# Zeros ahead of the first h, x loaded by head on two queues, half the state later: the head of a fused attention and gated-MLP kernel

## The chip, the cores and the metric

One core of one Trainium2 chip. The metric is the device time of one execution in microseconds (us), the median of several runs. Ratios between two kernels are the mean time of one kernel's runs over that of the other's of the same rounds, so they are not quite the ratios of the medians quoted beside them.

## The reference, cut to what matters

```python
def _attn_ref(x, state):                      # x (8, 8, 512, 64), state (8, 8, 32, 64)
    scores = scale * np.matmul(x, state.transpose(0, 1, 3, 2))
    a = softmax(scores);   xread = np.matmul(a, state)
    scores2 = scale * np.matmul(state, x.transpose(0, 1, 3, 2))
    a2 = softmax(scores2); sread = np.matmul(a2, x)
    return np.concatenate([xread, sread], axis=2)

def _moe_ref(x, w_in, w_out):                 # 4352 tokens, 512 -> 2048 -> 512
    h = x @ w_in
    g = h * np.cos(h)
    return g @ w_out
```

(Softmax is abbreviated.) The weights come as 64-bit floats. The kernel turns them into 32-bit floats by handling their halves as integers, in the steps called 1, 2, a, b, c, d below.

## The kernel before: the parts concerned

Every engine works through a fixed order. A sample is one of the eight x[b]; before TensorE can make the first h of a sample, x must be loaded, turned by TensorE, multiplied with the state (scores), passed through a softmax on VectorE and ScalarE, and the first weights must be converted. Names used below: st is the state as loaded and stT the state turned and scaled; xT is x turned; aT is the result of the first softmax, which the first h needs; exp2 is the exponential of the second softmax (scores2), on ScalarE; q holds ScalarE's and VectorE's steps from h to g; a gate is the last of these (g_all from h and q). One `matmul` of the program shows as one or two passes in the trace, so a product of zeros is two passes. "By head" means by attention head; "the head of the kernel" is its first 130 us.

```python
    def load_x(b):                                   # four quarters of the tokens
        src = x[b].rearrange("h (c p) d -> c p h d", p=P)
        for c in range(NC):
            nc.sync.dma_start(out=x_b[:, c], in_=src[c])
    load_x(0)
    for k in range(NK):                              # the whole state, 8 loads of 64 KB
        for j in range(2):
            queue = nc.scalar if j == 0 else nc.gpsimd
            queue.dma_start(out=st[Ns * k:Ns * k + Ns, :, D * j:D * j + D], in_=st_src[j, k])
    # ... cut ...
        def all_tokens(self):                        # 16 transposes, k-major
            for k in range(NK):
                for c in range(NC):
                    self.turn_x(k, c, xp[k])
                # copied to xT[:, k] by ScalarE (k even) or VectorE (k odd)
    # ... cut ...
    fetch(3)                                         # first three weight loads, sync queue
    a0.all_tokens()
    states(0, at[0]); states_kept(0, at[0])          # the state's transposes, kept by VectorE
    a0.scores()
    convert(0, "12ab")                               # 1, 2: ScalarE; a, b, c: VectorE; d: GpSimd
    a0.max1(); a0.spread1(); a0.shift()
    convert(1, "12")
    a0.exp1()
    convert(0, "cd")
    a0.sums()
    convert(1, "abcd")                               # load 1: d on VectorE too
    a0.spread1()
    convert(2, "12")
    a0.norm1()                                       # aT is done: the first h can start
    a0.products(0, MAIN, 0, HC)
    # ... then 8 samples of 16 steps each: hidden (h), gate (q, g), output (o)
```

## Time and profile before

| | before |
|---|---|
| time, median of 6 runs | 821.85 us (821.24 to 821.96) |
| span in the profile | 819.9 us, granted clock 0.997 |
| TensorE busy | 765.5 us, 93% |
| scores start | 15.49 us |
| first h starts | 29.23 us |
| TensorE bound from | about 130 us |

In the busy rows of a page each digit is the busy share of a fortieth of the span, in tenths. A line of the chain of waits is start, duration, what; a line of the timeline is start, duration, engine, source line, operation, output and inputs, and in brackets how long the engine had been idle and what ended that.

### The profile page before, as it was taken

How to read it: one execution, taken by the hardware profiler on the slowest of the kernel's cores; microseconds unless marked ns; L12 is line 12 of the kernel's file. 1: busy time of each engine (PE TensorE's matmuls, PEld its weight loads, DVE VectorE, ACT ScalarE, POOL GpSimd, SP SyncE). 2: the span in 40 equal slices, each digit the busy share in tenths (PEclk: the TensorE clock that was granted, in tenths of full speed). 3: DMA queues.
4: the chain of work that ended last, by engine and by line, in shares of the span. 5: the costliest groups of instructions: out<-in, count | busy, mean ns of one | idle time of the engine just before them, and what ended most of it. 6: DMA issues, size and time to landing. Idle time of an engine off the chain costs nothing.

```text
span 819.9 us, 7479 instructions
## 1 busy us (share of the span) xinstructions
PE 765.5 (93%) x2720; PEld 345.0 (42%) x2720; DVE 434.6 (53%) x672; ACT 397.9 (49%) x644; POOL 175.6 (21%) x117
## 2 busy tenths in 40 slices
PE   3569688989999999999999999999999999999997
PEld 2133233434444444444444444444344444455554
DVE  2799897653355435863454456743554355432431
ACT  2568675564447344644455454634473445322222
POOL 1134236877100000154000000451000002620200
PEclk9999999999999999999999999999999999999999
DMA  6574450102000211030010311120000112200021
GB/s 154 179 203 158 153 154 0 27 0 52 1 13 14 52 26 26 13 65 0 1 26 1 64 21 19 26 52 0 14 14 0 27 26 50 79 0 14 13 39 38
DMA packets 110500, 37.18 MB, mean 45 GB/s; under 512 B 102464, under 2 KB 102464, under 8 KB 110464
## 3 DMA queue, kind: packets, MB, share of 16 engines
q1 hardware_dynamic: 109248, 36.19, 18.8%
q10 hardware_dynamic: 1088, 0.26, 0.2%
q8 instruction: 21, 0.34, 0.2%
q0 software_dynamic: 128, 0.26, 0.2%
q14 instruction: 15, 0.12, 0.1%
HBM read 27.79 MB, written 8.91 MB: 45 GB/s over the span
## 4 chain that ended last, share of the span: by engine, by line
PE 78%; DVE 12%; ACT 7%; issue 1%; DMA 1%; POOL 0%; SPq 0%; DVEq 0%; POOLq 0%
PE o L489 42%; PE h L424 25%; PE at L276 4%; PE o L606 3%; DVE q L433 2%; PE at L363 2%; ACT q L439 1%; DVE g_all L445 1%; PE at L249 1%; ACT q L438 1%; DVE w_in L211 1%; DVE w_out L211 1%; DVE xT L296 1%; DVE aT L340 1%; DMA x_b<-in_x_dram 1%
## 5 line engine op out<-in xcount | busy, mean ns | idle before, releaser
L424 PE MATMUL h<-aT,sw 128*128 128x512 f32 x512 | 244.0, 599 | 17.9 <-DVE g_all L445 14.1
L489 PE MATMUL o<-g_all,w_out 128*128 128x512 f32 x512 | 236.5, 598 | 5.5 <-DVE sw L403 2.9
L430 ACT ACTIVATE q<-h 128x512 f32<-128x512 f32 (+1 forms) x144 | 82.2, 571 | 269.6 <-PE h L424 269.6
L451 POOL TENSOR_TENSOR g_all<-g_all 128x512 f32<-128x512 f32 x80 | 112.1, 1424 | 460.1 <-DVE g_all L445 454.5
L433 DVE SCALAR_TENSOR_TENSOR q<-q,h 128x512 f32<-128x512 f32 (+1 forms) x144 | 94.3, 655 | 208.0 <-ACT q L430 208.0
L489 PE MATMUL o<-g_all,s 128*128 128x512 f32 x384 | 177.3, 598 | 0.0
L445 DVE TENSOR_TENSOR g_all<-h,q 128x512 f32<-128x512 f32 (+1 forms) x144 | 94.8, 658 | 139.7 <-ACT q L439 139.4
L424 PEld LDWEIGHTS h<-aT,sw 128*128 128x128 f32 x512 | 96.6, 191 | 145.5 <-issue 109.3
L489 PEld LDWEIGHTS o<-g_all,w_out 128*128 128x128 f32 x512 | 93.6, 190 | 127.3 <-issue 119.8
L438 ACT ACTIVATE q<-q 128x512 f32<-128x512 f32 (+1 forms) x144 | 87.6, 608 | 103.6 <-DVE q L433 103.6
L489 PEld LDWEIGHTS o<-g_all,s 128*128 128x128 f32 x384 | 70.3, 190 | 88.4 <-issue 83.6
L439 ACT ACTIVATE q<-q,halfpi 128x512 f32<-128x512 f32 (+1 forms) x144 | 100.5, 698 | 4.5
L222 POOL TENSOR_TENSOR w_out<-w_out,s 128x1024 int32<-128x1024 int32 x10 | 23.8, 2385 | 87.5 <-DVE w_out L216 76.3
L451 DVE TENSOR_TENSOR g_all<-g_all 128x512 f32<-128x512 f32 x48 | 33.2, 692 | 1.6
L424 PE MATMUL h<-sT,w_in 128*128 128x256 f32 x128 | 30.2, 379 | 0.0
L405 ACT COPY sw<-at 128x512 f32<-128x512 f32 x48 | 25.7, 588 | 9.0 <-PE at L276 9.0
L606 PE MATMUL o<-w_out,g_all 128*128 128x512 f32 x64 | 29.6, 592 | 0.0
L222 POOL TENSOR_TENSOR w_in<-w_in,s 128x1024 int32<-128x1024 int32 (+1 forms) x9 | 18.0, 2000 | 53.8 <-DVE w_in L216 53.8
L424 PEld LDWEIGHTS h<-sT,w_in 128*128 128x128 f32 x128 | 24.3, 190 | 10.1 <-issue 6.7
L495 DVE SCALAR_TENSOR_TENSOR held<-o,held 128x512 f32<-128x512 f32 x40 | 25.5, 681 | 3.7 <-PE o L489 3.7
L276 PE MATMUL at<-w_in,stT 64*32 64x512 f32 x384 | 26.1, 601 | 0.0
L276 PE MATMUL o<-w_in,stT 64*32 64x512 f32 (+1 forms) x144 | 13.0, 606 | 13.3 <-POOL w_in L222 11.1
(79 smaller groups left out, 468.4 us busy)
## 6 DMA issues: line engine op xcount, KB each, us to landing
out_dram<-ot SPq DMA_DIRECT2D x136, 64.0 KB, 2.0
x_b<-in_x_dram SPq DMA_DIRECT2D x32, 256.0 KB, 4.5
g_all<-in_moe_w_out_dram SPq DMA_DIRECT2D x8, 1024.0 KB, 5.0
g_all<-in_moe_w_in_dram SPq DMA_DIRECT2D x6, 1024.0 KB, 5.3
g_all<-in_moe_w_in_dram SPq DMA_DIRECT2D x4, 512.0 KB, 7.0
x_b<-in_moe_w_out_dram SPq DMA_DIRECT2D x1, 1024.0 KB, 6.3
xT<-in_moe_w_out_dram SPq DMA_DIRECT2D x1, 1024.0 KB, 8.3
s<-in_state_dram ACTq DMA_DIRECT2D x4, 64.0 KB, 5.1
```

The lines of the kernel that those rows point to most:

```text
L222: engine.tensor_tensor(bits, bits, e.bitcast(I32), op=ALU.add)
L276: nc.tensor.matmul(out=(to or at)[j][Ns * k:Ns * k + Ns, 0:n], lhsT=w[D * j:D * j + D, self.b, Ns * k:Ns * k + Ns], rhs=r(slice(D * j, D * ...
L405: nc.scalar.copy(dst, to[j][:, 0:c1 - c0])
L424: nc.tensor.matmul(out=t.hp, lhsT=t.lhs(i), rhs=t.rhs(i), start=(i == 0), stop=(i == t.kn - 1))
L430: nc.scalar.activation(t.q, t.hp, func=ACTF.Copy, bias=MAGIC)
L433: nc.vector.scalar_tensor_tensor(out=t.q, in0=t.q, scalar=MAGIC, in1=t.hp, op0=ALU.subtract, op1=ALU.subtract)
L438: nc.scalar.activation(t.q, t.q, func=ACTF.Abs)
L439: nc.scalar.activation(t.q, t.q, func=ACTF.Sin, bias=halfpi, scale=-TWO_PI)
L445: nc.vector.tensor_tensor(t.g, t.hp, t.q, op=ALU.mult)
L451: engine.tensor_tensor(out, a, b, op=ALU.subtract)
L489: nc.tensor.matmul(out=acc[bank][ch], lhsT=w[:, i, P * ch:P * ch + P], rhs=g.g, start=(i == 0), stop=(i == NH - 1))
L606: nc.tensor.matmul(out=acc[MAIN][i], lhsT=t.g[:, P * i:P * i + P], rhs=w_out[:, :, t.f, :], start=(n == 0), stop=(n == NF - 1))
```

## The change

Its intent: have x and the needed part of the state earlier, work on each pair of heads as it lands, use VectorE's gap before the softmax sums for the second weight load, and keep TensorE's clock up ahead of the first h.

```diff
-    def load_x(b):
-        src = x[b].rearrange("h (c p) d -> c p h d", p=P)
-        for c in range(NC):
-            nc.sync.dma_start(out=x_b[:, c], in_=src[c])
-    load_x(0)
+    def load_x(b, queues):
+        src = x[b].rearrange("h (c p) d -> p c h d", p=P)
+        for h in range(H):
+            queues[h % 2].dma_start(out=x_b[:, :, h], in_=src[:, :, h])
+    zeros = g_all[:, 0]
+    nc.vector.memset(zeros, 0.0)
+    load_x(0, (nc.sync, nc.scalar))
...
+    def load_state(half, queues):                    # 4 of 8 samples, 8 loads of 32 KB
+        ...
+                queues[j].dma_start(out=st[..., b, ...], in_=st_src[j, k, :, b])
+    load_state(0, (nc.scalar, nc.gpsimd))
...
-            nc.vector.tensor_scalar(dst, dst, 2.0 ** -15, None, op0=ALU.max)
+            engine = nc.gpsimd if i == 1 else nc.vector
+            engine.tensor_scalar(dst, dst, 2.0 ** -15, None, op0=ALU.max)
...
-            engine = nc.vector if i == 1 else nc.gpsimd
-            engine.tensor_tensor(bits, bits, e.bitcast(I32), op=ALU.add)
+            n = 1 if i < 4 else 2
+            for j in range(n):
+                r = slice(m * j // n, m * j // n + m // n)
+                nc.gpsimd.tensor_tensor(bits[:, r], bits[:, r], e.bitcast(I32)[:, r], op=ALU.add)
...
     fetch(3)
+    load_state(1, (nc.sync, nc.sync))
+    warm(2, at[0])                                   # products of zeros
     a0.all_tokens()
     states(0, at[0]); states_kept(0, at[0])
     a0.scores()
+    warm(6, acc[SIDE][1])
     convert(0, "12ab")
+    convert(1, "12a")
     a0.max1(); a0.spread1(); a0.shift()
-    convert(1, "12")
     a0.exp1()
     convert(0, "cd")
+    convert(1, "bcd")
     a0.sums()
-    convert(1, "abcd")
     a0.spread1()
```

More of the change, by code (lines that the diff above doesn't have):

```diff
@@ L102 @@
     stT = consts.tile([P, B, P], F32)
-    def load_x(b):
-        src = x[b].rearrange("h (c p) d -> c p h d", p=P)
-        for c in range(NC):
-            nc.sync.dma_start(out=x_b[:, c], in_=src[c])
-    load_x(0)
-    st_src = state.rearrange("b (k j) n d -> j k n b d", j=2)
-    for k in range(NK):
-        for j in range(2):
-            queue = nc.scalar if j == 0 else nc.gpsimd
-            queue.dma_start(
-                out=st[Ns * k:Ns * k + Ns, :, D * j:D * j + D],
-                in_=st_src[j, k])
+    def load_x(b, queues):
[5 more added lines that the diff above has]
+    load_x(0, (nc.sync, nc.scalar))
+    st_src = state.rearrange("b (k j) n d -> j k n b d", j=2)
+    def load_state(half, queues):
+        b = slice(4 * half, 4 * half + 4)
+        for k in range(NK):
+            for j in range(2):
+                queues[j].dma_start(
+                    out=st[Ns * k:Ns * k + Ns, b, D * j:D * j + D],
+                    in_=st_src[j, k, :, b])
+    load_state(0, (nc.scalar, nc.gpsimd))
     at = [aps.tile([P, S], F32, name=f"at{j}") for j in range(2)]
@@ L220, in convert_part @@
         else:
-            engine = nc.vector if i == 1 else nc.gpsimd
-            engine.tensor_tensor(bits, bits, e.bitcast(I32), op=ALU.add)
+            n = 1 if i < 4 else 2
+            for j in range(n):
+                r = slice(m * j // n, m * j // n + m // n)
+                nc.gpsimd.tensor_tensor(bits[:, r], bits[:, r],
+                                        e.bitcast(I32)[:, r], op=ALU.add)
     sT = consts.tile([P, NK, B, Ns], F32)
@@ L414, in part @@
         if (name, args) == ("reads", (1,)) and b + 1 < B:
-            load_x(b + 1)
+            load_x(b + 1, (nc.sync, nc.sync))
     class Tile:
@@ L646, in tiles, with warm @@
             yield t
+    def warm(n, to):
+        for _ in range(n):
+            nc.tensor.matmul(out=to, lhsT=zeros[:, 0:P], rhs=zeros, start=True,
+                             stop=True)
     fetch(3)
+    load_state(1, (nc.sync, nc.sync))
+    warm(2, at[0])
     a0 = attn[0] = Attention(0)
```

## The prediction

> **What bounds the kernel now.** I read the busy row by slices first, then the chain that ended last in order of time, then the instructions of the first 130 us, then the same window cut into stretches.
>
> ```profile
> PE   3569688989999999999999999999999999999997
> DVE  2799897653355435863454456743554355432431
> ...
> PE 78%; DVE 12%; ACT 7%; issue 1%; DMA 1%; POOL 0%; SPq 0%; DVEq 0%; POOLq 0%
> ```
>
> A slice is 20.5 us. From the seventh slice on (about 130 us) TensorE is the bound: it works 632.83 of the 640 us after 180. The change hardly touches that part; it can only move it earlier as a whole. What can be won lies before 130 us, where TensorE is a third to two thirds busy. The chain of waits there starts so (start us, us, what):
>
> ```profile
> 3.05 7.64 DMA x_b<-in_x_dram
> 10.68 0.04 issue
> 10.73 3.04 PE o L249 x13
> 13.76 0.87 PE at L129 x4
> 14.63 0.02 issue
> 14.65 0.70 DVE stT L135
> 15.36 0.14 issue
> 15.49 2.06 PE at L276 x16
> 17.55 1.31 DVE m L290 x2
> ```
>
> The end hangs on the last quarter of x (landed at 10.7), then on 13 transposes that all waited for it, the state's transposes, the scores, and then VectorE without a hole until the first h:
>
> ```profile
> 22.57 1.30 DVE L290 TRANSPOSE_TENSOR_REDUCE m<-aT 128x16 f32<-128x512 f32 x2 [0.53 <-ACT aT L317]
> ...
> 24.39 0.36 DVE L211 TENSOR_SCALAR w_in<-w_in 128x512 f32<-128x512 f32 x1
> 24.79 0.43 DVE L213 TENSOR_SCALAR w_in<-w_in 128x512 int32<-128x512 int32 x1
> 25.25 0.69 DVE L216 SCALAR_TENSOR_TENSOR w_in<-g_all,w_in 128x512 int32<-128x512 int32 x1
> 25.98 0.69 DVE L222 CUSTOM_DVE_ANT_0 w_in<-w_in,s 128x1024 uint16<-128x1024 uint16 x1
> ...
> 27.86 1.23 DVE L340 TENSOR_TENSOR aT<-aT,xT 128x1024 f32<-128x1024 f32 x1
> ...
> 29.23 5.52 PE L424 MATMUL h<-aT,sw 128*128 128x512 f32 x8 [1.43 <-DVE aT L340]
> ```
>
> The four lines at 24.39 to 26.67 are the second weight load's conversion, standing between the softmax sums and the division; VectorE stood idle 0.53 us just before the sums, for the exponential. The first h matmuls: 8 take 5.52 us, while later four take 1.98 us, so some five of them ran at half speed.
>
> From 29 to 130 us the chain goes through VectorE, ScalarE and GpSimd in turn (all three run fixed orders), TensorE seldom. One group stands out:
>
> ```profile
> L211 DVE TENSOR_SCALAR w_in<-w_in x10: 363/682/2396, 15.3 to 83.2; 128x1024 f32<-128x1024 f32 x6, 128x512 f32<-128x512 f32 x4
> ```
>
> The same instruction takes 0.68 us alone and up to 2.4 us beside GpSimd's add: at 42.76 it took 2.37 us, ending 0.55 us after the add (42.21, 2.37 us).
>
> **What the Trainium skill says.** "TensorE: Matmul & The Clock Gate", Part 1: the array runs at half rate when it was idle and speeds up after about 3.4 us of sustained work. The trace agrees: 0.85 us apart at first, 0.43 us from 33.3, some 4 us in. "SBUF — State Buffer", Who interferes with whom: a VectorE instruction in a two-port mode, or with two SBUF inputs, and a GpSimd one exclude each other for the whole of the first to start. L211's 2.37 us shows it. "DMA: Bandwidth & Descriptors", Issuing engines are not separate DMA queues: a second issuing engine saves only issue time. In the stretches 2 to 9.5 us the 16 engines show a share of 1.02 to 1.32 at 230 to 182 GB/s, so they were full; I count nothing for the second queue as such.
>
> **The change part by part.**
>
> 1. Half of the state later. Until 9.5 us the stretches moved 1.57 MB (2 us each at 230, 214 and 206 GB/s, 1.5 us at 182), exactly x (1.05) and state (0.52), and x was seen 1.2 us after. Now x must share only with GpSimd's quarter of the state, 0.13 MB (ScalarE's quarter is queued behind its x): 1.18 MB at the same 213 GB/s is 5.5 us from 2.0, so 7.5, and seen at 8.75. Gain 1.9 us, an estimate. The first weights are then seen at about 10.9.
>
> 2. By head. A pair of heads gives four transposes at once; after the last pair only 4 of 0.234 us remain where 13 did: 9 x 0.234 = 2.1 us. So the scores start at about 11.5 instead of 15.49, and end at 13.5 instead of 17.53. ScalarE issues four x loads and four state loads first (0.55 us each, 4.4 us), then loads its table (1.28 us); it is free by 6.5, before its first copy.
>
> 3. Second conversion in gaps. Before, from the end of the scores to the end of L340 it is 29.09 - 17.53 = 11.56 us. Its max goes to GpSimd, its add too; shift (0.43) and xor (0.69) go before the sums, of which the exponential's wait hides 0.53 us. 0.36 + 0.43 + 0.69 + 0.69 with gaps (2.2) goes out of the path and 0.6 comes in: 1.6 us gained. But both adds (1.27 us each) now run on GpSimd just when VectorE does the shift, the xor and the small add after the sums (L332), which need the same port; each can be held up to 1.27 us. Laying them in order by "who comes first keeps it" gives an end between 9.95 and 11.3 us after the scores. I take 10.7: gain 0.9 us.
>
> 4. Zeros. Two products (four passes of 0.85 us at the slow clock) run at about 1.3 to 4.7 us, while x is awaited: free. Six (12 passes) start behind the scores, some five to seven at 0.85 and the rest at 0.43: about 7.5 us, until 21. The first real products can start when the first add ends, about 20, and the second half needs the second add, about 22; I count no delay. The first h then runs at full speed, saving 5 x 0.43 = 2.1 us of TensorE. But that isn't on the path: h was ready at about 32.6, ScalarE took it only at 33.42, behind exp2, which hangs on VectorE. I count 0. If the two early products keep the clock up through the scores, those take 1.09 instead of 1.96 us: 0.87 us at one chance in three, 0.3 us.
>
> 5. The add of the 14 full loads, and of the two late ones, in halves. Each now costs 2 x 1.27 instead of 2.37 us. A waiting L211 gets the port after 1.26 us. At 186.09 a tiny VectorE add took 0.36 us beside nine GpSimd instructions in a row, so VectorE does get in at such a border. Five L211 (42.76, 48.52, 56.92, 108.20, 126.56) came early enough in the add to profit. If VectorE then keeps the port for L213 too, each saves 1.0 us, less about 1.5 us where the chain hangs on the add itself (47.74 to 50.12): 3 us gained. If GpSimd gets it back in between, L213 waits for the second half and each loses 0.24 us, and that add ends 0.8 us later: 2 us lost. I take 0.5 us gained.
>
> 6. x loads of later samples: eight issues of about 0.4 us in place of four of 0.58, asked for at 52.76 and used at 61.93: hidden.
>
> Sum: 1.9 + 2.1 + 0.9 + 0.3 + 0.5 = 5.7 us. The first h should start at about 24.2 instead of 29.23. As every later step up to 130 us hangs on the same orders, and the weight loads (5 us) are asked for steps ahead, I let nearly all of it through and take off 0.4 us for what is lost on the way: 821.8 - 5.3 = 816.5.
>
> **Rivals.** (a) The transfer is hidden or the state becomes the wait: st now lies behind x in ScalarE's queue, and if it lands after 10 us, the state's transposes wait. For it: 0.13 MB more at 213 GB/s is 0.6 us. Against it: it is used only after x's last transposes, 0.94 us later. It would take 1 us: 817.5. (b) The conversions become the wait: L211 of load 0 stands in VectorE's order before the max, so weights landing after 12.5 would hold the softmax, and both adds on GpSimd hold L332. It would leave only parts 1 and 2, half eaten: 819. (c) Halving goes badly, or the slow clock falls elsewhere. At 50.16 eight matmuls took 1.93 instead of 1.06 us after a hole of 3.6 us; with a later add the hole grows: 819 to 820. (d) Everything goes well, the port stays with VectorE and the clock stays up: 811 to 813. (e) The zeros delay the real products: their 12 passes at 0.85 us would end at 23.7, a micro-second or two late: 818.
>
> **Range and chances.** The head gives 3 to 6 us, the halves -2 to +3: 812.5 to 819.5. For over 2% it would have to be under 805.4, more than the head has holes for; slower than 838 nothing suggests. Faster 0.02, same 0.97, slower 0.01.
>
> **What would show it.** Part 1: last x seen at 8 to 9.5 us. Part 2: four transposes after it, scores starting near 11.5. Part 3: L340 ending 10 to 11.3 us after the scores. Part 4: h at 0.43 us a pass, and ScalarE's first q still behind exp2. Part 5: L211 near 1.2 us or less where it took 2.4, and L213 either at 0.69 or at 1.9 us. Wrong I am, if the lead at the first h is not the lead at 130 us and at the end.

## More of the kernel before

The source lines of the changed kernel are shifted: its L264 is L249 of before (x's transposes), L138 was L129 (the state's), L291 was L276 (scores and weight products), L221, L223, L226, L236 were L211, L213, L216, L222 (steps a, b, c, d), L305 was L290 (max), L355 was L340 (aT), L439 was L424 (h). L667 is the new product of zeros.

## The result, and the profile after

The changed kernel takes 820.74 us (820.2 to 821.5, 6 runs) against 821.85; the ratio is 0.9989, with a 95% interval of 0.9976 to 1.0002. The forecast was 816.5 in 812.5 to 819.5. So 1.1 us came instead of 5.3, and the measured median lies outside the range. The interval includes 1, so even the 1.1 us is not clear of the noise.

The chain of waits of the changed kernel shows where the head now hangs:

```profile
1.85 5.22 DMA x_b<-in_x_dram
7.07 0.02 issue
7.09 0.32 ACTq L123
7.41 0.04 issue
7.45 4.94 DMA s<-in_state_dram
12.39 0.14 issue
12.52 1.10 PE at L138 x4
...
14.49 2.06 PE at L291 x16
```

x is no longer the wait. ScalarE's state loads stand behind x in its queue. In the chain the issue at 7.09 follows the landing of a load of x at 7.07; the last of them goes out at 7.45, takes 4.94 us for 32 KB, and lands at 12.39. TensorE had turned the last of x long before, as the timeline of the changed kernel shows in its first line here:

```profile
8.43 0.66 PE L264 MATMUL o<-ident,x_b 128*128 128x128 f32 x4 [0.66 <-DMA x_b<-in_x_dram]
...
20.96 0.42 DVE L223 TENSOR_SCALAR w_in<-w_in 128x512 int32<-128x512 int32 x1
...
21.41 1.65 DVE L226 SCALAR_TENSOR_TENSOR w_in<-g_all,w_in 128x512 int32<-128x512 int32 x1
...
26.22 1.23 DVE L355 TENSOR_TENSOR aT<-aT,xT 128x1024 f32<-128x1024 f32 x1
...
27.59 6.51 PE L439 MATMUL h<-aT,sw 128*128 128x512 f32 x8 [2.42 <-DVE aT L355]
...
54.26 2.93 POOL L236 TENSOR_TENSOR w_out<-w_out,s 128x512 int32<-128x512 int32 x2 [5.39 <-DVE w_out L226]
54.76 1.32 DVE L221 TENSOR_SCALAR w_in<-w_in 128x1024 f32<-128x1024 f32 x1
56.11 1.64 DVE L223 TENSOR_SCALAR w_in<-w_in 128x1024 int32<-128x1024 int32 x1
```

The only transposes left after the last of x are four (0.66 us), as forecast. The xor of load 1 (L226) takes 1.65 us instead of 0.69, because it stands beside GpSimd's add. The first h runs no faster: 6.51 us for the eight passes that took 5.52. And with the add in halves the max (L221) gets in after 1.3 us instead of 2.4, but then the shift (L223) waits for the second half, 1.64 us instead of 0.69.

Then the clock. The column of the granted clock can't be taken alone: it reads 1.00 for the first 30 us of the kernel before, while the transposes there took 0.23 us each and the first h's passes 0.85 us, the slow rate. So I go by the lengths of the matmuls. These are two stretches of the changed kernel's windows (the columns are the stretch, its length, busy time of each engine with counts, the granted clock of TensorE, the DMA share and GB/s), around the first h of the second sample:

```profile
122.00:124.80 2.80, 0.17 (x1) 0.00 (x0) 2.71 (x6) 2.18 (x3) 0.57 (x1) 1.00 0.00 0
124.80:128.00 3.20, 3.13 (x5) 1.12 (x5) 3.17 (x4) 0.00 (x0) 2.36 (x2) 0.61 0.00 0
```

After a hole of 2.7 us that h takes 3.22 us, in a stretch with a mean clock of 0.61. In the kernel before the same h came after a hole of 2.4 us, at full clock. First the changed kernel, then the kernel before:

```profile
124.86 3.22 PE L439 MATMUL h<-aT,sw 128*128 128x512 f32 x4 [2.69 <-DVE g_all L460]
...
126.70 1.98 PE L424 MATMUL h<-aT,sw 128*128 128x512 f32 x4 [2.38 <-DVE g_all L445]
```

To see where a lead is won and lost I take VectorE's gate multiplications (g from h and q, the 1st, 4th, 15th and 18th) as milestones. Their starts in the kernel before are 37.64, 56.31, 125.95 and 137.27 us. The lead is that time minus the same in the other kernel's trace:

| kernel | scores start | lead at 1st | at 4th | at 15th | at 18th | span shorter by |
|---|---|---|---|---|---|---|
| the change | 14.49 | 1.67 | 2.16 | 1.83 | 1.24 | 1.3 |

The lead at the 18th, at about 136 us, is nearly the lead at the end, because from there on TensorE is the bound and does the same work: in all twelve traces after the kernel before's, the span is shorter by that lead to within 0.5 us. One thing makes the lead at the 4th look better than it is: the kernel before's own trace ran at the slow clock at 50 us (eight matmuls in 1.93 us at 50.16), the change's did not.

### The profile page after: what moved, and what is told of

Its sections match the earlier page's. It is cut to its first block, busy times and chain, and to the rows that moved or that the text cites. A ratio compares the mean times of both kernels' runs of the same rounds, so it can differ in the third digit from the quotient of the medians.

```text
span 818.6 us, 7603 instructions
## 1 busy us (share of the span) xinstructions
PE 779.7 (95%) x2736; PEld 349.9 (43%) x2736; DVE 435.0 (53%) x671; ACT 397.6 (49%) x644; POOL 184.0 (22%) x135
## 4 chain that ended last, share of the span: by engine, by line
PE 78%; DVE 11%; ACT 7%; issue 1%; DMA 1%; POOL 0%; ACTq 0%; DVEq 0%; POOLq 0%
PE o L504 42%; PE h L439 25%; PE at L291 4%; PE o L621 3%; DVE q L448 2%; PE at L378 2%; ACT q L454 1%; PE at L264 1%; DVE g_all L460 1%; ACT q L453 1%; DVE xT L311 1%; DVE aT L355 1%; ACT xT L337 1%; DVE w_in L226 1%; DVE w_in L221 1%
## 5 line engine op out<-in xcount | busy, mean ns | idle before, releaser
L439 PE MATMUL h<-aT,sw 128*128 128x512 f32 x512 | 247.8, 607 | 16.4 <-DVE g_all L460 11.9
L236 POOL TENSOR_TENSOR w_out<-w_out,s 128x512 int32<-128x512 int32 x20 | 27.2, 1379 | 84.8 <-DVE w_out L226 80.0
L236 POOL TENSOR_TENSOR w_in<-w_in,s 128x512 int32<-128x512 int32 x16 | 21.7, 1369 | 37.7 <-DVE w_in L226 37.7
L531 DVE STREAM_TRANSPOSE ot<-held 128x512 f32<-128x512 f32 x32 | 22.2, 694 | 0.0
```

Source lines behind the costliest of these rows:

```text
L236: nc.gpsimd.tensor_tensor(bits[:, r], bits[:, r], e.bitcast(I32)[:, r], op=ALU.add)
L439: nc.tensor.matmul(out=t.hp, lhsT=t.lhs(i), rhs=t.rhs(i), start=(i == 0), stop=(i == t.kn - 1))
```

## The experiments

All runs gave correct results. Medians are of five runs each; "before" ran, nine runs each, on three chips, and gave 821.79, 821.84 and 821.97. The intervals of the ratios are some 0.0025 wide, 2 us. The milestones of all eleven are from one trace each; in e4, e5, e7, e9 and e10 the traced run was the slowest of the five, 0.4 to 1.5 us above the median, so a lead and a median need not match there.

| run | median us | ratio to before | scores start | lead at 1st | 4th | 15th | 18th |
|---|---|---|---|---|---|---|---|
| e1 state on GpSimd's queue | 820.86 | 0.9988 | 13.65 | 2.51 | 2.04 | 1.70 | 1.83 |
| e2 no zeros | 820.32 | 0.9983 | 14.30 | 1.84 | 2.33 | 1.98 | 1.33 |
| e3 whole adds | 820.54 | 0.9983 | 14.51 | 1.61 | 1.50 | 1.48 | 1.46 |
| e4 conversion as before | 822.25 | 1.0004 | 14.35 | 1.14 | 0.62 | 0.06 | -0.54 |
| e5 state on the sync queue | 816.42 | 0.9936 | 10.89 | 5.21 | 4.52 | 4.37 | 3.77 |
| e6 two bursts | 819.54 | 0.9973 | 14.32 | 1.82 | 2.29 | 1.98 | 2.11 |
| e7 e5 and a bridge | 816.42 | 0.9938 | 11.17 | 5.10 | 4.70 | 4.37 | 3.78 |
| e8 e5, bridge, bursts | 815.72 | 0.9929 | 11.00 | 5.17 | 5.64 | 5.12 | 5.25 |
| e9 weights after the state | 819.98 | 0.9977 | 12.56 | 2.02 | 1.63 | 1.47 | 0.88 |
| e10 e5, x by quarters | 818.59 | 0.9956 | 12.56 | 4.43 | 4.02 | 3.67 | 3.07 |
| e11 e8 with whole adds | 816.47 | 0.9935 | 10.91 | 6.07 | 6.36 | 5.82 | 5.81 |

The theories when I began: A, that the state has taken x's place as the wait of the head and that this alone explains the shortfall; B, its rival, that any lead at the first h is lost again before 130 us, because TensorE's clock falls elsewhere.

**e1, the state on another queue.** An edit to the change:

```diff
-    load_state(0, (nc.scalar, nc.gpsimd))
+    load_state(0, (nc.gpsimd, nc.gpsimd))
```

> The change with one edit: both halves of the early state go out on GpSimd's own queue, none behind x on ScalarE's. Theory A (three of the four us predicted for the head are lost because the state's first half is issued late behind x and lands at 12.4): the state lands by 9.5, the scores start at 11.5 to 12 instead of 14.49, the first h at about 25 instead of 27.59, and the time falls by about 2.5 us below the change (818.3). Rival B (a lead at the first h is lost again before 130 us, whatever its size, as the slow clock falls differently): the first h is earlier as well, but the time stays within 0.7 us of the change (820 to 821.4).

Rival B got what it expected: the first h came earlier, at 26.74, and the time stayed between 820 and 821.4. Theory A did not: the state's last load went out at 5.49 and still landed only at 11.55, so its queue was not the whole story. The lead grew by 0.84 us at the first gate, and nothing of that was left at the 4th.

**e2, no zeros.**

```diff
-    warm(2, at[0])
-    warm(6, acc[SIDE][1])
```

> The change without its eight products of zeros. If the zeros are worth nothing, as predicted, because the first h is not on the path: first h at 27.6 as before, at 0.85 us a pass in both, time within 0.5 us of the change (820.2 to 821.2). Rival B (the zeros shift the clock's windows, and with that come the slow h at 124.9 and the slow stretches of 64-76 and 94-106): mean clock back to 0.99 or more, and time 1 us or more below the change (819.7 or less). If the zeros help: time over 821.7.

820.32 us, 0.4 us under the change, within the spread of both. The first h ran 6.37 us, at the slow clock as well, and the h at 124.7 was slow too (3.55 us). So the eight products of zeros neither help nor are they what makes the later h slow. Half of what rival B expected came, a granted clock of 0.991 in all five runs (0.981 to 0.990 in the change's); but the time did not fall to 819.7 and the slow h stayed, so in its form "the zeros cause the slow h" it fell.

**e3, whole adds.**

```diff
-            n = 1 if i < 4 else 2
+            n = 1
```

> The change with GpSimd's add of a full load as one instruction again. If the halves are neutral (GpSimd takes the port back after the max, and the shift waits instead: 1.3 + 1.65 us where it was 2.4 + 0.7): time within 0.5 us of the change. If the halves cost by later ends of the adds (2.97 instead of 2.37 us): 0.7 us or more less than the change. If they gain: 0.7 us or more above it.

820.54 us: no difference that the intervals could show, as its first guess said. VectorE's 39 instructions of the steps a and b add up to 38.5 us in both traces: what the max gains, the shift loses.

**e4, the second conversion as before.** The max and the add of load 1 on VectorE, and the order of before:

```diff
-    convert(1, "12a")
     a0.max1(); a0.spread1(); a0.shift()
+    convert(1, "12")
     a0.exp1()
     convert(0, "cd")
-    convert(1, "bcd")
     a0.sums()
+    convert(1, "abcd")
```

> The change with the second load's conversion as before: its max and add on VectorE, all of it after the sums. Scores to the end of aT should be 11.6 us again instead of 10.9, so the first h at 28.2 instead of 27.6, and the time 0.6 us above the change if a lead carries through; unchanged if Rival B holds.

The first h started at 28.09, 0.5 us after the change's, and the time was 1.5 us above the change's (with overlapping intervals): the conversion in gaps is worth its 0.5 us at the first h. The other 1 us appears between the 1st and the 4th gate, where this trace has TensorE at the slow clock from 48 to 54 us and the change's trace has not. That led to theory C: the clock falls in TensorE's holes, at one of two places where TensorE is on the path (48 to 54 us, and 123 to 128 us), and each costs up to 1 us.

**e5, the state in front of the weights.** One word of the change:

```diff
-    load_state(0, (nc.scalar, nc.gpsimd))
+    load_state(0, (nc.sync, nc.gpsimd))
```

> The change with ScalarE's half of the early state moved to the sync queue, between x and the weights, so that the weights stand behind it there. Theory A2 (the state is late because 1.5 MB of weights now run beside it on the same 16 engines, not because of the queue's order alone): the state lands by about 9.5, the scores start at 11.5 to 12, the first h at 24.6 to 25. If GpSimd's other half is what lands late, the scores start after 13 again, as with the state on GpSimd's queue (13.65). The time: 818.5 if the lead carries through, 820 or more if the slow clock takes it back.

816.42 us, a ratio of 0.9936 (0.9922 to 0.9949), and 4.3 us below the change. Its chain of waits:

```profile
5.14 0.31 SPq L123
5.45 0.04 issue
5.50 3.75 DMA s<-in_state_dram
9.25 0.14 issue
9.39 0.64 PE at L138 x4
...
10.89 2.06 PE at L291 x16
```

The state lands at 9.25 instead of 12.39, the scores start 3.6 us earlier and so do all milestones; 0.6 to 0.7 us of the lead is lost at each of the two slow places in this trace. Theory A holds in its second form, and rival B in its strict form falls: most of a lead goes through to the end. Even here the state is what the scores wait for: the last transposes of x start at 8.21, and the state lands at 9.25.

**e6, the clock held at two places.** Three products ahead of the products of step 3 and three ahead of the second sample's first h, into accumulators that are free at that time and overwritten after:

```diff
+        if step == NF:
+            keep_warm(3, acc[MAIN][0])       # product of stT and the identity
         hidden(t)
+        if step == 3:
+            keep_warm(3, acc[SIDE][1])
```

> The change with two bursts of three more products (into banks that are free then, so results stay right), one ahead of the products of step 3 (about 47 us), one ahead of the first h of the second sample (about 123). Theory C (TensorE's clock drops in holes of 2.4 to 3.6 us, and where it lies on the path it costs about 1 us each time): h at 124.9 takes 1.98 instead of 3.22 us, the lead at 131 us is 1.8 to 2.2 instead of 1.1, the time 0.7 to 1 us below the change (819.7 to 820.1). If the slow h is not what loses the lead: time unchanged. If the bursts stand in the way: time above the change.

819.54 us (819.41 to 819.64), every run below every run of the change (820.2 and up), though the intervals of the two ratios overlap. Its timeline at the place in question:

```profile
122.08 2.74 PE L673 MATMUL o<-stT,ident 128*128 128x512 f32 x6
124.71 1.98 PE L439 MATMUL h<-aT,sw 128*128 128x512 f32 x4
```

The burst fills the hole, h takes 1.98 us instead of 3.22, and the lead at the 18th is 2.11 instead of 1.24. The other traces bear it out. In the ten without a burst at this place h was slow (2.95 to 3.55 us) in seven, among them the change, e5 and e7, and took 1.98 us in three (before, e1, e3). The lead fell by 0.6 us from the 15th to the 18th gate in all seven; in e1, e3 and the three with a burst (e6, e8, e11) it held. So theory C is shown for this place, at 0.6 us. As some traces without a burst kept the clock too, one trace alone would not show that the burst did it.

**e7, a bridge to the first h.** e5 and three more products of zeros behind the first real products:

```diff
     a0.products(0, MAIN, 0, HC)
+    warm(3, acc[SIDE][1])
```

> The run before last with three more products of zeros right behind the first real products, so that no hole of 2.4 us stands before the first h. By my step 4 the first h is not on the path: eight passes take 3.5 us instead of 5.4 to 6.5, ScalarE's first q still starts behind exp2, and the time is the same within 0.5 us as with the state on the sync queue alone. If the first h is on the path after all: 1 us or more below it.

The eight passes took 3.60 instead of 5.37 us; ScalarE took the first q at 28.32, in e5 at 28.17, both right behind exp2; the time was 816.42 in both. By itself this is no test of the clock: the bridge also held h back from 23.98 to 25.72, so it ended at the same time, 29.3, in both. e8 settles it. There the bridge did not hold h back (24.29 to 27.89), h ended 1.5 us sooner than in e5, and the first gate came no sooner (32.47 against 32.43). The first h is not on the path.

**e8, all together** (e5, the bridge and the two bursts):

> All three together. If the head's lead and the clock are the whole story: first h at 24.6 to 25, no slow clock on the path up to 131, and the lead there 3.5 to 4.5 us, time 817.3 to 818.3. If the lead is eaten by a third thing: above 819.5.

815.72 us (815.06 to 816.52), 6.1 us below the kernel before, ratio 0.9929 (0.9916 to 0.9941). The lead is 5.17 us at the first gate and 5.25 at the 18th. It expected 817.3 to 818.3: the direction was right, and the lead larger, because the scores started at 11.0 and neither of the two places was slow. Against e5's 816.42 the 0.7 us are within the intervals; the traces differ by 1.5 us at the 18th gate.

**e9, the weights later, the state where the change has it.**

```diff
-    fetch(3)
     load_state(1, (nc.sync, nc.sync))
+    fetch(3)
```

> The change with two lines swapped: the state's second half is asked for ahead of the weights on the sync queue, so the weights start later; the state's first half stays on ScalarE's queue behind x. If the 1.5 MB of weights beside it are what holds the state's first half: it lands by about 10 instead of 12.4 and the scores start near 11.5. If its own late issue behind x on ScalarE's queue (the last one went out at 7.5) is what holds it: it still lands at 12 and the scores start near 14. In both, the first weights land later, by 12 to 13, and may hold the max behind them.

The last two lines here are from two other views of the same run: when ScalarE issued the state's loads (the first and the last start), and the state's transposes.

```profile
3.98 5.24 DMA s<-in_state_dram
...
11.02 3.62 DMA g_all<-in_moe_w_in_dram
14.64 0.02 issue
14.66 0.67 ACT w_in L214
...
16.24 1.23 DVE m L305 x2
...
L123 ACTq DMA_DIRECT2D s<-in_state_dram x4: 318/322/344, 4.0 to 8.5; - x4
...
10.61 1.09 PE L138 MATMUL at<-ident,s 128*128 128x128 f32 x4 [1.44 <-DMA s<-in_state_dram]
```

The state's transposes started at 10.61 instead of 12.52. So with the weights out of its way the state came 1.9 us sooner from the same queue. It did so although ScalarE's last load of it went out 1 us later than in the change (8.5 instead of 7.45): from issue to the transposes it took 2.1 us here and 5.1 us there. So the traffic of the weights made up about 3 us of the load's flight, and what is left of its lateness against e5's 9.39 goes with the late issue: in e5 the last one of these went out on the sync queue at 5.50. Whether the state's second half, which was issued in turn with it here, made the issue later still, this run cannot tell. As feared, the weights then landed at 14.64 and held the max.

**e10, x by quarters** (e5 with the loads of x as in the kernel before, on two queues):

```diff
-        for h in range(H):
-            queues[h % 2].dma_start(out=x_b[:, :, h], in_=src[:, :, h])
+        for c in range(NC):
+            queues[c % 2].dma_start(out=x_b[:, c], in_=src[c])
```

> The version with ScalarE's state on the sync queue (816.4, scores at 10.89), but x by quarters of the tokens as in the kernel before, still on two queues. By my step 2 the load by head saves 9 transposes of 0.234 us: the scores should start 1.5 to 2.1 us later, at 12.4 to 13, and the time be 1.5 to 2 us higher, about 818.2. If the load by head is worth nothing: 816.4.

```profile
8.05 3.04 PE L264 MATMUL o<-ident,x_b 128*128 128x128 f32 x13 [0.58 <-DMA x_b<-in_x_dram]
...
12.56 1.09 PE L291 MATMUL at<-xT,stT 64*32 64x512 f32 x16 [1.02 <-DVE stT L144]
```

Thirteen transposes wait for the last of x again, the scores start 1.67 us later than in e5, and the time is 2.2 us higher, at 818.59. At the scores' start the load by head is worth about what step 2 said; at the transposes of x, which end at 11.09 here and at 8.87 in e5, it is worth 2.2 us. The time says it less cleanly: the scores happened to run at full clock here (1.09 instead of 1.96 us), the lead at the gates is only 0.5 to 0.8 us below e5's, and the intervals overlap.

**e11, e8 with whole adds.**

> The version with the state on the sync queue, the bridge and the two bursts (815.72), but GpSimd's adds whole. With the clock held, the halves' own worth should show: if each L221-L223 pair beside halves takes longer than beside one whole add (2.97 against 2.67 us), 0.3 to 0.8 us less than 815.72; if they help, as much above it; neutral within 0.3 us if early max and late shift cancel.

816.47 us against 815.72, with overlapping intervals of the ratios (0.9923 to 0.9948 and 0.9916 to 0.9941), and spans of 814.5 and 814.6 us in the two profiles. The halves' own worth stays open: the medians are 0.75 us apart, the intervals 2 us wide. e11's larger lead at the first gate (6.07 against 5.17) goes with scores at full clock, not with the adds.

## Why the prediction was wrong, point by point

**The step that failed is step 2's "the scores start at about 11.5", with rival (a)'s price for a late state.** The prediction saw the state behind x in ScalarE's queue and priced its lateness as "0.13 MB more at 213 GB/s is 0.6 us", at most 1 us in all. The state landed at 12.39 and cost 3.0 us: the scores started at 14.49. Two things were mis-sized. One is the issue: eight issues of 0.55 us should have been done 4.4 us in, ScalarE free by 6.5; but they waited for x to land, the last load of the state went out at 7.45, and ScalarE had loaded its table only at 9.20 (hidden here, behind the state). The other is the flight: 4.94 us for 32 KB, because the sizing took x and the state as alone on the 16 DMA engines. With only half of x on the sync queue, the weights behind it moved sooner, beside the 32 KB loads: by the traces' semaphores the first weight load had landed at 9.8, in the kernel before at 12.05; in the kernel before, the weights had stood behind all of x and so, as it happened, behind the state. The prediction had worked out that x and the state moved alone until 9.5 us, and did not ask what that order rested on. e9 takes the weights away and the flight shrinks to about 2 us; e5 puts the state in front of the weights, and earlier out, by one word, and its scores start at 10.89 with a time of 816.42.

**Step 1, x seen at 8.75: right.** The last four transposes started at 8.43.

**Step 2, 9 transposes saved: right in itself.** Between e10 and e5 it is 2.2 us at the end of x's transposes and 1.67 at the scores, where 2.1 was said. In the change it was hidden behind the state.

**Step 3, 10.7 us from the end of the scores to the end of aT: right.** It was 27.45 - 16.54 = 10.91, with the xor held beside the add as described (1.65 us). e4 gives 0.5 us of first-h start for it.

**Step 4, zeros worth nothing through the first h: right,** though not for the whole reason given. They did not even speed it up: the clock fell again in the hole of 2.4 us behind the first real products, and h took 6.51 us. e8 shows that h ending 1.5 us sooner does not move the first gate. The hoped-for full clock in the scores (1.09 instead of 1.96 us) did not come in the change's trace; of the ten experiments with zeros it came in three (e7, e10, e11).

**Step 5, halves: the second branch came,** with GpSimd taking the port back between the max and the shift (1.32 and 1.64 us). The forecast of 2 us lost for that branch was too dark: e3's median is 0.2 us away and VectorE's time for the two steps is the same, 38.5 us.

**"Nearly all of it through", minus 0.4 us: wrong in size.** The change reached 2.2 us of lead at the 4th gate and came home with 1.2 to 1.3. The largest term is the slow clock at the second sample's first h (3.22 instead of 1.98 us), 0.6 us of lead. Rival (c) named the clock, but laid it to the place at 50 us and to later adds. e6 shows it at 124.9.

The balance against the forecast lead of 5.3 us: 3.0 for the state, 0.2 in step 3, 0.3 for the scores' clock that did not come, and 0.6 between the 15th and the 18th gate, together 4.1 of the 4.2 us missing. That it closes so well is in part luck: the 0.5 us won from the 1st to the 4th gate, where the kernel before's trace was slow, stands in the place of the 0.5 us counted for the halves, and the 0.3 us lost from the 4th to the 15th, unexplained here, in that of the 0.4 us taken off. The small rest, and how often the clock falls at each of the two places, would need more than one trace of each kernel.

## What to carry to other kernels

When a load is made earlier, ask what stands behind it in the same queue, because that comes earlier as well and may overtake something small that is needed first. Put what is needed first ahead of the bulk in the bulk's own queue, where the order keeps it in front. And where TensorE waits on the path between bursts (here for some 2.5 us), look at the length of the next matmuls: a few spare products in the hole were worth 0.6 to 1.2 us at the second sample's first h, while the same spare products ahead of an h that nobody was waiting for were worth nothing.

## What the Trainium skill lacked or had wrong

- "TensorE: Matmul & The Clock Gate", HAM oscillation: it warns of idle gaps beyond some 3.4 us. Here shorter ones were enough: 2.42 us before the first h, and 2.46 to 2.69 us before the second sample's first h in seven traces, while gaps of 2.38, 2.40 and 2.48 us there kept the clock in three. So the length of the gap alone did not decide it.
- "TensorE: Matmul & The Clock Gate", Part 4, says that the full clock does not engage for transposes in the array's transpose mode. The same four transposes of the state took 1.10 us in the change and 0.64 us in e5, where TensorE had been busy just before; so these ran at either rate. Whether the hardware's transpose mode was on for them, no trace here shows.
- "DMA: Bandwidth & Descriptors", Issuing engines are not separate DMA queues, says that a second issuing engine saves issue time only. That section lacks the other side: what a load stands behind in its queue, and what then runs beside it. Moving 0.13 MB of state from ScalarE's to the sync queue, ahead of the weights, changed its landing from 12.39 to 9.25 us and the time by 4.3 us.
- "SBUF — State Buffer", Who interferes with whom, says that who issues first keeps the shared port for the whole instruction, but not who gets it next when both sides have work waiting. Here it changed hands at each instruction, as the lengths suggest: max 1.32 us, second half of the add, then the shift, 1.64 us.
